# q and k of the first two units: vector-engine transposes replaced by tensor-engine transposes in a chunk attention + gated MLP kernel

## The chip, the cores and the metric

The kernel runs on one core of one Trainium2 chip. The metric is the device time of one execution in microseconds (us). The engines are TensorE (PE; PEld is its weight load), VectorE (DVE), ScalarE (ACT), GpSimd (POOL) and SyncE (SP). SP and POOL issue the DMAs here: SP on queue q1, POOL on queue q0.

## The reference

Chunk attention without a causal mask over chunks of 64 positions, then a two-layer MLP with a swish that has its own beta for each hidden unit. Batch 8, 8 heads, 576 positions, head size 64; 4608 tokens, model width 512, hidden width 2048, all float32.

```python
scores = scale * np.matmul(q_c, k_c.transpose(0, 1, 2, 4, 3))   # (B, H, 9, 64, 64)
scores = scores - np.max(scores, axis=-1, keepdims=True)
attn = np.exp(scores)
attn = attn / (np.sum(attn, axis=-1, keepdims=True) + 1e-09)
out = np.matmul(attn, v_c)
...
x = np.ascontiguousarray(attn_out.transpose(0, 2, 1, 3)).reshape(B * S, H * D)
h = x @ w_in
g = h * (1.0 / (1.0 + np.exp(-beta * h)))
return (g @ w_out).astype(np.float32)
```

## The kernel before

**Units and blocks.** The 4608 tokens are cut into 18 units of 256, and two units make a block of 512 for the MLP. A unit goes through these steps: load q, k and v (all converted to float16); transpose q and k, so that the head dimension lies in the partitions; scores in PSUM (a tile `sc`); exponential on ScalarE (`et`, L208 for units 0 and 1); product with v, which carries a column of ones so that the row sum comes with it (`emit_pv`, L266); reciprocal and multiplication on VectorE (`emit_norm`, L285 and L287); TensorE transposes of the normalized output into `xp` (L303), and a copy to `xt` (L304). `emit_m` (L329, L339, L343) then makes one of 16 hidden pieces of 128: four matmuls into `hps`, a tanh on ScalarE into `sg`, and one VectorE instruction that makes `gt` from both (a swish written with a tanh). `emit_t` (L361, L371) multiplies `gt` with w_out, and the result goes out.

**Order.** The order of each engine's instructions is the order of the calls in the text, written out by hand; each engine runs its own in order, and waits are set by the framework from the tiles that are read and written. PSUM tiles come from three pools: `ps_p`, four banks in turn (tag "p"), and `ps_s` and `ps_x`, two banks each, one tile at a time (tags "s" and "x").

**Units 0 and 1** are treated apart, since nothing else can run until they are done. Their q and k are loaded together, 512 tokens, four tokens to a partition, and by halves of the heads (a = 0 and 1, four heads each). Half 0 comes on SP's queue as float32 (`raw0`) and is cast on ScalarE (L178); half 1 comes on POOL's queue, which converts it to float16 (`qk0[1]`, named h in the profile). `emit_T_half` (L174) transposes with VectorE, which works on 32x32 blocks; taken on pairs of float16, this leaves 32 partitions with two interleaved elements, so `emit_sc_half` (L186) needs two accumulating matmuls over 32 rows for each score tile of 64x64: 32 matmuls for a unit and a half. `emit_ex_half` (L206) takes the exponential. After half 0 of unit 0, the scores of both units' other halves follow, then `emit_pv(0)` and `emit_pv(1)`, and the first pieces of `emit_m` on columns 0 to 256 (the tokens of unit 0), four of them, with the transposes of unit 1's output in between. Then the same four pieces on columns 256 to 512 (unit 1), and from there pieces of 512 columns. `gt` of these first pieces is made where the calls `vec()` stand.

**Fillers.** `emit_tiny` and `emit_idle` are matmuls on zeros that only keep TensorE busy. One matmul reads `late`, which POOL sets after two loads of v, so that the fillers behind it don't start before that.

**POOL's queue** is issued in this order: q and k of half 1 (L401), v in pieces of 128 tokens (L113; pieces 0 and 1 belong to unit 0, 2 and 3 to unit 1), the identity for the TensorE transposes (two POOL instructions in masks.py), eight pieces of w_in (L131), w_out (L137) and then unit after unit. An issue waits until the one eight before it has landed. **SP's queue**: q and k of half 0 (L401), beta in four pieces (L407), and later the outputs.

**Unit 2** is placed in the second layer of block 0, which runs as 16 chunks (i) of four matmuls each: its scores ahead of chunk 8, its product ahead of chunk 10, the transposes of its output ahead of chunk 13.

Of the kernel before, what the change touches and what calls it, by code (L numbers as in the profile page):

```python
# [8 lines left out]
FP32 = mybir.dt.float32  # L9
# [6 lines left out]
def kernel(  # L16
# [45 lines left out]
    qkT0 = [[const.tile([128, HH, 128, 2], FP16, name=f"t0{i}{a}") for i in range(2)] for a in range(2)]  # L62
# [111 lines left out]
    def emit_T_half(a):  # L174
        for i, h0, h1 in ((0, 0, HH), (1, 0, HH // 2), (1, HH // 2, HH)) if a == 0 else ((0, 0, HH), (1, 0, HH)):
            src = qk0[a][i][:, h0:h1]
            if a == 0:
                nc.scalar.copy(out=src, in_=raw0[i][:, h0:h1])  # L178
            nc.vector.transpose(
                out=qkT0[a][i][:, h0:h1].rearrange("p h s e -> p (h s e)").bitcast(FP32).rearrange(  # L180
                    "p (h i r) -> p h r i", h=h1 - h0, r=4),
                in_=src.rearrange("p h r d -> p (h r d)").bitcast(FP32).rearrange(
                    "p (h r i) -> p h r i", h=h1 - h0, r=4),
            )

    def emit_sc_half(u, a):  # L186
# [5 lines left out]
        qt, kt = qkT0[a]  # L192
        for h in range(HH):
            for e in range(2):
                for s in range(2):
                    p0 = 64 * u + 32 * s
                    for c in range(2):
                        nc.tensor.matmul(  # L198
                            out=sc[64 * c:64 * c + 64, s, HH * a + h, :],
                            lhsT=kt[p0:p0 + 32, h, 64 * c:64 * c + 64, e],  # L200
                            rhs=qt[p0:p0 + 32, h, 64 * c:64 * c + 64, e],
                            start=(e == 0),
                            stop=(e == 1),
                        )

    def emit_ex_half(u, a, n=1):  # L206
        hs = slice(HH * a, HH * (a + n))
        nc.scalar.activation(  # L208
            out=et_t[u][:, :, hs], in_=x_t["sc", u][:, :, hs], func=ACTF.Exp, scale=scale)
# [44 lines left out]
    def emit_pv(u, where=("x", "s")):  # L254
        et = et_t.pop(u)
        for s in (1, 0) if u >= MU else (0, 1):
# [137 lines left out]
    with tc.manual_schedule():  # L394
# [13 lines left out]
        for i in range(4):  # L408
            load_v(i)
            if i == 1:  # L410
                nc.gpsimd.memset(late, 0.0)
        nxt[0] = 2
        make_identity(nc, ident)
        for g in range(8):
            load_w_in(g)
# [230 lines left out]
```

The softmax here doesn't subtract the row's maximum and nothing guards it: scores larger than these inputs give would overflow.

## Time and profile before

| | us |
|---|---|
| median of 12 runs | 288.13 |
| lowest, highest | 287.24, 289.14 |
| profiled execution, its own time | 287.64 |
| its span in the profile | 285.9 |

The span runs from the first instruction of the program to the last that the profiler recorded, and is 1.74 us shorter than the execution's own time. Times inside the profile are us from the start of the span. A line of the timeline has start, length, engine, line of the kernel, operation, the tile written and the tiles read, the shape, the number of instructions that were merged, and in brackets how long the engine stood idle before it and what ended that. The chain of waits is the work that ended last, followed back from the end; its lines have start, length, engine, tile and line. In the DMA view a line for a queue has packets, megabytes, and the time of its packets as a share of the 16 DMA engines' time in the window.

### The profile page before, as it was taken

The numbers are of one execution on the slowest core, as the hardware profiler recorded it, in microseconds if no ns is written. First come the engines' busy times: TensorE is split into PE (matmuls) and PEld (weight loads), VectorE is DVE, ScalarE is ACT, GpSimd is POOL, SyncE is SP. The second block draws the span as 40 slices with busy tenths as digits, with TensorE's granted clock in tenths as the row PEclk, the third lists the DMA queues.
The fourth block names the chain that finished last, engine by engine and source line by source line (L and its number), as shares of the span: only waits on it lengthen the run. The fifth ranks groups of instructions, "written<-read, shape, count | busy, mean of one in ns | idle before, by whom it ended". The sixth has DMA issues, their size and how long they took to land.

```text
span 285.9 us, 6671 instructions
## 1 busy us (share of the span) xinstructions
PE 279.0 (98%) x2779; PEld 136.1 (48%) x2779; DVE 143.9 (50%) x268; ACT 146.3 (51%) x223; POOL 95.7 (33%) x125
## 2 busy tenths in 40 slices
PE   6989999999999999999999999999999999999995
PEld 3564456544544444444444444444444444444444
DVE  2778444776558553535454536363635463333301
ACT  4478228773557545455554555554645444444411
POOL 8853678488073991258627000000000000000000
PEclk9999999999999999999999999999999999999999
DMA  8999999999999999999999993425311221010012
GB/s 194 176 197 206 181 180 213 209 166 149 205 96 185 177 176 175 159 145 175 197 161 177 156 169 78 100 57 119 86 48 39 73 57 55 37 39 37 37 73 76
DMA packets 141085, 37.40 MB, mean 131 GB/s; under 512 B 128000, under 2 KB 136576, under 8 KB 141056
## 3 DMA queue, kind: packets, MB, share of 16 engines
q0 software_dynamic: 99136, 17.83, 79.0%
q1 hardware_dynamic: 41776, 19.09, 33.2%
q8 instruction: 22, 0.36, 0.5%
q10 hardware_dynamic: 144, 0.07, 0.1%
q14 instruction: 7, 0.06, 0.1%
HBM read 36.71 MB, written 9.44 MB: 161 GB/s over the span
## 4 chain that ended last, share of the span: by engine, by line
PE 94%; DMA 3%; ACT 1%; issue 1%; DVE 0%; POOL 0%; DVEq 0%; POOLq 0%
PE hps L329 44%; PE ops L361 43%; DMA h<-in_k_dram 3%; PE x L266 2%; PE sc L238 1%; PE ops L602 1%; PE sc L225 1%; PE y L266 1%; ACT xt L304 1%; PE xp L303 0%; PE sc L198 0%; ACT et L208 0%; POOL h L401 0%; PE warm L381 0%; PE xp L311 0%
## 5 line engine op out<-in xcount | busy, mean ns | idle before, releaser
L343 DVE SCALAR_TENSOR_TENSOR gt<-sg,hps 128x512 f16<-128x512 f32 (+1 forms) x153 | 99.2, 655 | 102.0 <-ACT sg L339 101.2
L329 PE MATMUL hps<-xt,win 128*128 128x512 f16 (+1 forms) x612 | 136.2, 367 | 0.8 <-ACT xt L304 0.7
L339 ACT ACTIVATE sg<-hps,beta 128x512 f32<-128x512 f32 (+1 forms) x153 | 100.4, 663 | 71.2 <-PE hps L329 69.5
L361 PE MATMUL ops<-wout,gt 128*128 128x512 f16 x560 | 131.1, 379 | 0.0
L329 PEld LDWEIGHTS <-win 128*128 128x128 f16 x612 | 58.1, 98 | 62.7 <-issue 1.4
L361 PEld LDWEIGHTS <-gt 128*128 128x128 f16 x560 | 54.1, 98 | 64.1
L371 ACT ACTIVATE osb<-ops 128x512 f32<-128x512 f32 x35 | 20.9, 598 | 42.7 <-PE ops L361 42.7
L113 POOL DMA_DIRECT2D vbig<-in_v_dram x40 | 34.1, 868 | 12.0 <-DMA qu<-in_q_dram 4.7
L99 POOL DMA_DIRECT2D qu<-in_q_dram x22 | 18.7, 859 | 25.9 <-DMA qT<-qu 23.6
L287 DVE TENSOR_TENSOR x<-x,rd 128x512 f16<-128x512 f32 x27 | 18.7, 691 | 1.0
L99 POOL DMA_DIRECT2D ku<-in_k_dram x22 | 18.7, 871 | 1.0 <-DMA ku<-in_k_dram 0.9
L285 DVE RECIPROCAL rd<-x 128x8 f32<-128x8 f32 x27 | 5.4, 199 | 12.6 <-PE x L266 12.6
L247 ACT ACTIVATE et<-sc 128x1024 f16<-128x1024 f32 (+1 forms) x8 | 6.4, 811 | 8.8 <-PE sc L238 8.7
L231 ACT ACTIVATE et<-sc 128x1024 f16<-128x1024 f32 x10 | 10.2, 1022 | 0.8 <-PE sc L225 0.2
L266 PEld LDWEIGHTS <-et 64*64 64x64 f16 x576 | 6.0, 107 | 7.4 <-issue 4.7
L287 DVE TENSOR_TENSOR x<-y,rd 128x256 f16<-128x256 f32 x18 | 7.6, 424 | 0.6
L381 PE MATMUL warm<-idle 128*128 128x512 f16 (+1 forms) x32 | 7.8, 396 | 0.0
L105 POOL DMA_DIRECT2D qu<-in_q_dram x9 | 6.8, 769 | 2.3 <-DMA vbig<-in_v_dram 0.8
L105 POOL DMA_DIRECT2D ku<-in_k_dram x9 | 6.8, 762 | 1.8 <-DMA win<-in_moe_w_in_dram 1.3
L266 PE MATMUL x<-vbig,et 64*64 64x65 f16 x432 | 6.7, 194 | 0.2 <-ACT et L208 0.2
L614 DVE TENSOR_SCALAR osb<-ops 128x256 f32<-128x256 f32 (+1 forms) x2 | 0.7, 358 | 12.1 <-PE ops L602 12.1
L131 POOL DMA_DIRECT2D win<-in_moe_w_in_dram x8 | 6.0, 758 | 1.2 <-DMA vbig<-in_v_dram 0.9
(46 smaller groups left out, 75.1 us busy)
## 6 DMA issues: line engine op xcount, KB each, us to landing
out_dram<-osb SPq DMA_DIRECT2D x35, 256.0 KB, 2.9
vbig<-in_v_dram POOLq DMA_DIRECT2D x32, 128.0 KB, 8.1
qu<-in_q_dram POOLq DMA_DIRECT2D x20, 128.0 KB, 6.2
ku<-in_k_dram POOLq DMA_DIRECT2D x20, 128.0 KB, 7.7
win<-in_moe_w_in_dram POOLq DMA_DIRECT2D x8, 256.0 KB, 8.8
wout<-in_moe_w_out_dram POOLq DMA_DIRECT2D x4, 512.0 KB, 12.5
qu<-in_q_dram POOLq DMA_DIRECT2D x3, 256.0 KB, 7.2
ku<-in_k_dram POOLq DMA_DIRECT2D x3, 256.0 KB, 7.8
```

Source lines behind the costliest of these rows:

```text
L99: nc.gpsimd.dma_start(out=tv[off:off + n, sp], in_=src[b, :, s:s + n, :].rearrange("h p d -> p h d"),)
L105: nc.gpsimd.dma_start(out=t[off // 2:(off + n) // 2], in_=src[b, :, s:s + n, :].rearrange("h (p r) d -> p h r d", r=2),)
L113: nc.gpsimd.dma_start(out=vbig[off:off + n, i, :, 0:D], in_=v[b, :, s:s + n, :].rearrange("h p d -> p h d"),)
L231: nc.scalar.activation(out=et, in_=sc, func=ACTF.Exp, scale=scale)
L266: nc.tensor.matmul(out=(x[0][64 * c:64 * c + 64, r, g, 0:D + 1] if len(x) == 1 else x[r][64 * c:64 * c + 64, g, 0:D + 1]), lhsT=(et[64 * r ...
L287: nc.vector.tensor_tensor(out=o, in0=z[..., 0:D], in1=rd[:, r].to_broadcast(list(o.shape)), op=ALU.mult)
L329: nc.tensor.matmul(out=hps[:, 0:n], lhsT=w_in16[m // 2][:, kk, (m % 2) * 128:(m % 2) * 128 + 128], rhs=xr[:, c0 // CH:(c0 + n) // CH, 2 * ...
L339: nc.scalar.activation(out=sg[:, 0:n], in_=hps[:, 0:n], func=ACTF.Tanh, scale=beta2[:, m:m + 1])
L343: nc.vector.scalar_tensor_tensor(out=gt_t[j][:, m, c0:c0 + n], in0=sg[:, 0:n], scalar=1.0, in1=hps[:, 0:n], op0=ALU.add, op1=ALU.mult,)
L361: nc.tensor.matmul(out=ops, lhsT=gt_t[j][:, kk, t * 128:(t + 1) * 128], rhs=w_out16[kk // 4][:, kk % 4, :], start=(kk == 0), stop=(kk == K ...
L371: nc.scalar.activation(out=osb, in_=ops, func=ACTF.Copy, scale=0.5)
L381: nc.tensor.matmul(out=d[:, 0:w], lhsT=idle[:, 0:128], rhs=idle[:, 0:w])
```

## The change

q and k of units 0 and 1 are transposed on TensorE, against the identity, one head and one of the four token positions at a time: 16 transposes of 128 x 64 for each of q and k and each half of the heads, 64 in all, into a PSUM tile `tq` that fills one bank. Even heads go to partitions 0 to 63, odd ones to 64 to 127. Two copies bring a tile to SBUF and put the tokens in order on the way: ScalarE takes heads 0 and 1 of the half (f = 0), VectorE heads 2 and 3 (f = 1). The casts of half 0 are shared in the same way. The scores need one matmul over 64 rows for each tile, 16 for a unit and a half instead of 32. `et` of units 0 and 1 is then ordered as it already is in units 8 and up, which `emit_pv` is told.

The identity is made first on POOL, `late` is set after one load of v instead of two, and piece 0 of w_in is issued ahead of v of unit 1. The fillers are placed anew. The product of unit 1 is split: its first part (s = 0) ahead of the first hidden pieces, its second part behind two of them; all four `vec()` of the first pieces now stand behind the transposes of unit 1's output. Unit 2's scores and product stand one chunk later (9 and 11).

```diff
--- before.py
+++ after.py
@@ -59,7 +59,7 @@
     HH = H // 2
     raw0 = [const.tile([128, HH, 4, D], FP32, name=f"raw{i}") for i in range(2)]
     qk0 = [[const.tile([128, HH, 4, D], FP16, name=f"h0{i}{a}") for i in range(2)] for a in range(2)]
-    qkT0 = [[const.tile([128, HH, 128, 2], FP16, name=f"t0{i}{a}") for i in range(2)] for a in range(2)]
+    qkT0 = [[const.tile([128, 2, 128, 4], FP16, name=f"t0{i}{a}") for i in range(2)] for a in range(2)]
     braw = const.tile([128, 32], FP32)
     gate = const.tile([128, 1], FP16)
     bt = const.tile([128, 32], FP32)
@@ -171,17 +171,25 @@
     x16_t = {}
     xt_t = {}
 
-    def emit_T_half(a):
-        for i, h0, h1 in ((0, 0, HH), (1, 0, HH // 2), (1, HH // 2, HH)) if a == 0 else ((0, 0, HH), (1, 0, HH)):
-            src = qk0[a][i][:, h0:h1]
-            if a == 0:
-                nc.scalar.copy(out=src, in_=raw0[i][:, h0:h1])
-            nc.vector.transpose(
-                out=qkT0[a][i][:, h0:h1].rearrange("p h s e -> p (h s e)").bitcast(FP32).rearrange(
-                    "p (h i r) -> p h r i", h=h1 - h0, r=4),
-                in_=src.rearrange("p h r d -> p (h r d)").bitcast(FP32).rearrange(
-                    "p (h r i) -> p h r i", h=h1 - h0, r=4),
-            )
+    tq_t = {}
+
+    def emit_cast_half(i, f, cast):
+        hs = slice(2 * f, 2 * f + 2)
+        cast(out=qk0[0][i][:, hs], in_=raw0[i][:, hs])
+
+    def emit_T_half(a, i):
+        z = tq_t[a, i] = ps_p.tile([128, 2, 4, 128], FP16, tag="p", name="tq")
+        for h in range(HH):
+            p0 = 64 * (h % 2)
+            for r in range(4):
+                nc.tensor.transpose(
+                    out=z[p0:p0 + 64, h // 2, r, :], in_=qk0[a][i][:, h, r, :], identity=ident)
+
+    def emit_cp_half(a, i, f, copy):
+        copy(
+            out=qkT0[a][i][:, f],
+            in_=tq_t[a, i][:, f].rearrange("p r t -> p t r"),
+        )
 
     def emit_sc_half(u, a):
         if a == 0:
@@ -189,24 +197,22 @@
             pool, tag = ((ps_s, "s"), (ps_x, "x"))[u]
             x_t["sc", u] = pool.tile([128, 2, H, CH], FP32, tag=tag, name="sc")
         sc = x_t["sc", u]
-        qt, kt = qkT0[a]
-        for h in range(HH):
-            for e in range(2):
-                for s in range(2):
-                    p0 = 64 * u + 32 * s
+        qt, kt = (z.rearrange("p g t r -> p g (t r)") for z in qkT0[a])
+        for s in range(2):
+            for g in range(2):
+                for par in range(2):
                     for c in range(2):
+                        t0 = UNIT * u + 128 * s + 64 * c
                         nc.tensor.matmul(
-                            out=sc[64 * c:64 * c + 64, s, HH * a + h, :],
-                            lhsT=kt[p0:p0 + 32, h, 64 * c:64 * c + 64, e],
-                            rhs=qt[p0:p0 + 32, h, 64 * c:64 * c + 64, e],
-                            start=(e == 0),
-                            stop=(e == 1),
+                            out=sc[64 * c:64 * c + 64, par, 4 * s + 2 * a + g, :],
+                            lhsT=kt[64 * par:64 * par + 64, g, t0:t0 + 64],
+                            rhs=qt[64 * par:64 * par + 64, g, t0:t0 + 64],
                         )
 
     def emit_ex_half(u, a, n=1):
-        hs = slice(HH * a, HH * (a + n))
-        nc.scalar.activation(
-            out=et_t[u][:, :, hs], in_=x_t["sc", u][:, :, hs], func=ACTF.Exp, scale=scale)
+        o, i = ((z.rearrange("p e (s g) q -> p (e s) g q", s=2)[:, :, 2 * a:2 * a + 2] if n == 1 else z)
+                for z in (et_t[u], x_t["sc", u]))
+        nc.scalar.activation(out=o, in_=i, func=ACTF.Exp, scale=scale)
 
     ex_t = {}
 
@@ -251,9 +257,9 @@
         while ex_t[u] and not later:
             emit_ex(u)
 
-    def emit_pv(u, where=("x", "s")):
-        et = et_t.pop(u)
-        for s in (1, 0) if u >= MU else (0, 1):
+    def emit_pv(u, where=("x", "s"), which=None):
+        et = et_t[u]
+        for s in which or ((1, 0) if u >= MU else (0, 1)):
             i = 2 * u + s
             if where[s] == "p":
                 x = [ps_p.tile([128, 4, 128], FP32, tag="p", name=f"y{r}") for r in range(2)]
@@ -266,7 +272,7 @@
                         nc.tensor.matmul(
                             out=(x[0][64 * c:64 * c + 64, r, g, 0:D + 1] if len(x) == 1 else
                                  x[r][64 * c:64 * c + 64, g, 0:D + 1]),
-                            lhsT=(et[64 * r:64 * r + 64, s, 4 * c + g, :] if u < XU else
+                            lhsT=(et[64 * r:64 * r + 64, s, 4 * c + g, :] if 2 <= u < XU else
                                   et[64 * r:64 * r + 64, g % 2, 4 * s + 2 * c + g // 2, :]),
                             rhs=vbig[64 * r:64 * r + 64, i, 4 * c + g, 0:D + 1],
                         )
@@ -297,7 +303,7 @@
 
     def emit_xt_pe(u, s, copy=nc.scalar.copy):
         xf = x16_t.pop((u, s)).rearrange("p r h d -> p (r h d)")
-        tag = "s" if u < 2 and (u, s) != (1, 0) else "xp"[s]
+        tag = ("ss", "sx")[u][s] if u < 2 else "xp"[s]
         xp = {"x": ps_x, "s": ps_s, "p": ps_p}[tag].tile([128, 4, 128], FP16, tag=tag, name="xp")
         for g in range(4):
             nc.tensor.transpose(out=xp[:, g, :], in_=xf[:, g * 128:(g + 1) * 128], identity=ident)
@@ -396,6 +402,7 @@
         nc.vector.memset(idle, 0.0)
         nc.vector.memset(braw, 0.0)
         nc.vector.memset(vbig[:, :, :, D:D + 1], 1.0)
+        make_identity(nc, ident)
         for a, eng, dst in ((0, nc.sync, raw0), (1, nc.gpsimd, qk0[1])):
             for i, src in enumerate((q, k)):
                 eng.dma_start(
@@ -405,13 +412,14 @@
         bv = moe_beta.rearrange("(m w f) -> w m f", w=4, f=32)
         for w in range(4):
             nc.sync.dma_start(out=braw[32 * w:32 * w + KFF, :], in_=bv[w])
-        for i in range(4):
-            load_v(i)
-            if i == 1:
-                nc.gpsimd.memset(late, 0.0)
+        load_v(0)
+        nc.gpsimd.memset(late, 0.0)
+        load_v(1)
+        load_w_in(0)
+        load_v(2)
+        load_v(3)
         nxt[0] = 2
-        make_identity(nc, ident)
-        for g in range(8):
+        for g in range(1, 8):
             load_w_in(g)
         for g in range(3):
             load_w_out(g)
@@ -419,47 +427,62 @@
         load_w_out(3)
         loads_to(3)
 
-        emit_tiny(78)
+        emit_tiny(75)
+        act_cp, vec_cp = nc.scalar.copy, nc.vector.tensor_copy
+        warm = idle_bank()
+        emit_idle(6, 512, warm)
+        nc.tensor.matmul(out=warm[:, 0:16], lhsT=idle[:, 0:128], rhs=late)
+        emit_idle(1, 512, warm)
+        for i in range(2):
+            emit_cast_half(i, 0, act_cp)
+            emit_cast_half(i, 1, vec_cp)
+        for i in range(2):
+            emit_T_half(0, i)
+            emit_cp_half(0, i, 0, act_cp)
+            emit_cp_half(0, i, 1, vec_cp)
+            if i == 0:
+                emit_idle(2, 512, warm)
+        emit_T_half(1, 0)
+        emit_cp_half(1, 0, 0, act_cp)
+        emit_cp_half(1, 0, 1, vec_cp)
+        emit_idle(1, 512, warm)
+        emit_sc_half(0, 0)
+        emit_ex_half(0, 0)
+        emit_sc_half(1, 0)
+        emit_T_half(1, 1)
+        emit_cp_half(1, 1, 0, act_cp)
+        emit_cp_half(1, 1, 1, vec_cp)
         warm = idle_bank()
         emit_idle(3, 512, warm)
-        nc.tensor.matmul(out=warm[:, 0:16], lhsT=idle[:, 0:128], rhs=late)
-        emit_idle(8, 512, warm)
-        emit_T_half(0)
-        emit_sc_half(0, 0)
-        emit_ex_half(0, 0)
-        warm = idle_bank()
-        emit_idle(6, 512, warm)
-        emit_T_half(1)
         nc.vector.transpose(out=bt, in_=braw)
         emit_sc_half(0, 1)
         emit_ex_half(0, 1)
-        emit_sc_half(1, 0)
+        emit_sc_half(1, 1)
+        emit_ex_half(1, 0, 2)
+        nc.scalar.activation(out=beta2, in_=bt[:, 0:KFF], func=ACTF.Copy, scale=0.5)
         emit_idle(2, 512, warm)
+        emit_idle(10, 64, warm)
         loads_to(5)
         emit_pv(0, ("s", "p"))
-        emit_sc_half(1, 1)
-        emit_ex_half(1, 0, 2)
         emit_norm(0, 0)
         emit_norm(0, 1)
-        emit_idle(1, 512, warm)
-        emit_idle(12, 64, warm)
+        emit_idle(4, 512, warm)
         emit_xt_pe(0, 0)
-        emit_pv(1, ("x", "p"))
-        emit_norm(1, 1)
+        emit_idle(4, 512, warm)
+        emit_xt_pe(0, 1)
+        emit_pv(1, ("p", "x"), (0,))
         emit_norm(1, 0)
-        nc.scalar.activation(out=beta2, in_=bt[:, 0:KFF], func=ACTF.Copy, scale=0.5)
-        emit_xt_pe(0, 1)
         d = [emit_m(0, m, 0, 256, True) for m in (0, 1)]
         d[0][0]()
-        emit_xt_pe(1, 1)
+        emit_pv(1, ("p", "x"), (1,))
+        emit_norm(1, 1)
         d[1][0]()
-        d.append(emit_m(0, 2, 0, 256, True))
-        d[0][1]()
-        emit_xt_pe(1, 0, nc.vector.tensor_copy)
-        d.append(emit_m(0, 3, 0, 256, True))
+        emit_xt_pe(1, 0)
+        d += [emit_m(0, m, 0, 256, True) for m in (2, 3)]
+        emit_xt_pe(1, 1, vec_cp)
         for act, _ in d[2:]:
             act()
-        for _, vec in d[1:]:
+        for _, vec in d:
             vec()
         for m in range(4):
             emit_m(0, m, 256, 256)
@@ -467,9 +490,9 @@
             emit_m(0, m)
         emit_T(2)
         for i in range(16):
-            if i == 8:
+            if i == 9:
                 emit_sc(2)
-            if i == 10:
+            if i == 11:
                 emit_pv(2)
                 emit_norm(2, 0)
                 emit_norm(2, 1)
```

## The prediction

> **What bounds the kernel now.** I read the page's head first, then the chain of waits over the first 30 us, then the timeline of the same stretch, then the DMA view by windows.
>
> From the page:
>
> ```profile
> span 285.9 us, 6671 instructions
> PE 279.0 (98%) x2779; PEld 136.1 (48%) x2779; DVE 143.9 (50%) x268; ACT 146.3 (51%) x223; POOL 95.7 (33%) x125
> ```
>
> TensorE is the bound, and its few idle times lie at the start: after its first instruction at 0.96 us it stands still for 2.6 us in all, 0.1 us of it after 17.6. So what counts is when TensorE begins to stream without a break. The chain of waits (start, length, what) shows that:
>
> ```profile
> 2.13 7.17 DMA h<-in_k_dram
> ...
> 10.46 0.71 PE sc L198 x62
> ...
> 15.14 1.03 PE hps L329 x8
> ...
> 17.57 12.28 PE hps L329 x64
> ```
>
> The last load of the first heads, h of k, lands at 9.30; scores start at 10.46, the first hidden layer (hps, L329) at 15.14, and from 17.57, the first of the 256:512 pieces (call it the stream), nothing stops TensorE. The work behind that point is the same in both kernels, so the change moves the end by what it moves 17.57. The prices come from the timeline (start, length, engine, line):
>
> ```profile
> 4.85 3.58 PE L381 MATMUL warm<-idle 128*128 128x512 f16 x8
> 6.11 1.14 ACT L178 CAST h<-raw 128x512 f16<-128x512 f32 x2 [0.44 <-DMA raw<-in_k_dram]
> 8.73 1.47 PE L381 MATMUL warm<-idle 128*128 128x512 f16 x6
> 9.32 1.09 DVE L179 STREAM_TRANSPOSE t<-h 128x512 f32<-128x512 f32 x1 [0.24 <-DMA h<-in_k_dram]
> 10.97 0.60 ACT L208 ACTIVATE et<-sc 128x512 f16<-128x512 f32 x1 [1.51 <-PE sc L198]
> 11.64 0.32 PE L266 MATMUL x<-vbig,et 64*64 64x65 f16 x16
> 13.01 0.40 PE L303 MATMUL xp<-ident,x 128*128 128x128 f16 x4
> 13.45 0.58 ACT L304 COPY xt<-xp 128x512 f16<-128x512 f16 x1
> 15.43 0.69 DVE L287 TENSOR_TENSOR x<-x,rd 128x512 f16<-128x512 f32 x1
> 16.67 0.39 PE L303 MATMUL xp<-ident,x 128*128 128x128 f16 x4
> 17.09 0.42 DVE L304 COPY xt<-xp 128x512 f16<-128x512 f16 x1 [0.33 <-PE xp L303]
> 17.43 3.03 DVE L343 SCALAR_TENSOR_TENSOR gt<-sg,hps 128x256 f16<-128x256 f32 x7
> ```
>
> **The loads.** Between 1.5 and 4.9 us the DMA view knows one queue only, that of the raw loads:
>
> ```profile
> q1 hardware_dynamic: 941, 0.95, 84.6%
> ```
>
> The h loads were issued at 1.24 and 2.13, yet not one of their packets ran by then. The change puts the identity ahead of them on POOL; its two instructions took 6.38 to 6.97, 0.59 us, so the h issues come at most 0.59 later. At 119.88, a later q load issued after its queue had run empty had its first packet by 122.41: 2.54 us. Then 1.83 + 2.54 = 4.37 is still inside the time of the raw loads, so I take 0, hidden by those; if the 3.69 us from issue to first packet were all the queue's own, it is +0.59. w_in piece 0 moves past the two v loads of unit 1: those land later (12.79 was the last; the 256 KB ahead of it cost 1.3, as between the landings at 14.09 and 15.42), 14.1 at worst, but are first used near 15.6. Piece 0 landed before its use already: 0 gained, and without that cover a late v would hold unit 1's products by its lateness. SP's queue is as before.
>
> **Up to the exponentials of unit 0's second half.** Before: landing 9.30, one DVE transpose 1.09, exp at 10.97, so 1.67 after the landing. The rest of the DVE transposes lay under the load. After: TensorE transposes, 16 of 64 columns a tile; four xp transposes took 0.40 and start 0.056 apart, so 16 take 15 x 0.056 + 0.22 = 1.06. Then two copies. The changed program's order has VectorE's copy wait for ScalarE's copy of the same tile, so they stand in line: 0.58 (the xt copy, same shape) plus, on VectorE, 0.42 (same shape, but contiguous) to 0.69 (512 results at L287's pace). The copy reads at a stride of 128 elements, so I take 0.69. Each hand-over costs about 0.03 to 0.05.
>
> TensorE is in order, and ahead of the last transposes stand both first-half scores, which need all of the raw k path: raw k lands 6.08, ScalarE's cast ends 6.72 (0.62 each; VectorE's half beside it), transposes 7.85, copies 8.45 and 9.2, 32 score tiles 0.3 (16 small matmuls of L266 take 0.32, starts over 0.15): 9.5. The transposes of k's last half run 9.5 to 10.56, copies to 11.2 and 11.9, its scores to 12.25, exp at 12.28. That is **+1.31**. On ScalarE the first exp (0.60) stands between these copies, from 9.65, behind the copy of h of q, to 10.3, so it is out of the way at 10.56; behind VectorE's waiting copy stand only the transpose of beta and the normalizing, not yet due. The bounds: with the two column groups overlapping (0.62 for 16) and 0.42 on VectorE, scores are out of the way at 8.8 and exp comes at 11.4, +0.4; with +0.59 on the load, 12.6, +1.7. Nothing waits for the transpose of beta until the first tanh.
>
> **From exp to the stream.** Exp 0.60, then pv of unit 0: before 10.97 to 11.64. In between the change has scores of unit 1 and fillers, 0.15 + 2 x 0.216 + 10 x 0.03 = 0.9 from 12.03: done at 12.9, just under 12.95. Then rec, multiply, xp, copy to xt, twice, to the first hps: 11.64 to 15.14, 3.50, which the change keeps (the eight fillers, 0.86 for each four, end about when VectorE does). First hps: 16.45. Behind that it is longer. Before, the products of unit 1 were done ahead of the first hps, and 17.57 came 2.43 later. After, two hidden pieces, 8 x 0.109 = 0.87, precede the second product; then 0.38 to its rec (11.64 to 12.02), 0.92 rec and multiply (15.20 to 16.12), 0.05 and 0.42 for xp (16.67 to 17.09), and copy plus the first gt, 0.76 (17.09 to 17.85), since all gt now stand behind that copy on VectorE and the stream's first bank is the first gt's: 3.4. **+1.0**, bounds +0.6 (no wait for gt) to +1.2.
>
> Sum: 1.31 + 1.0 = 2.3 on the profiled execution's own 287.64: 289.95. That execution was 0.49 under the median 288.13 of its runs. With the same distance 290.4; the new warm-up has no hole at 3.58, so a little of that distance may go: **290.3**. Pushing sc and pv of unit 2 one chunk back costs nothing: its kT and qT were ready at 35.7, 1.0 ahead, and a later stream adds to that; xp of unit 2 then follows pv by two chunks, 1.73 + 0.37 = 2.10, against 1.31 and 2.15 for the two multiplies (39.16 to 40.47 and 41.31), and the second is wanted 0.2 later. Without that cover, 0.3.
>
> **The clock.** Eight fillers from 4.85 took 3.58, six from 8.73 took 1.47: starts 0.43 and 0.216 apart, so the clock doubled near 8.3, after 3.5 us without a hole. After, the fillers run from 2.1 to 5.1 and then come transposes, so the sum above takes it as doubled by 7. Should it come only at 7.8, the raw k path is 0.5 later. If transposes did not bring it up at all, each 16 cost 1.8: 5.27, 7.05, fillers, 9.7, 11.5, 14.1, copies 15.5, exp 16.1, +5.1, and the halved pace of fillers and the first pieces another 1 to 2. No row of before shows a transpose on a slow clock.
>
> [...]
>
> **Rivals.** (1) The slow clock, 295: the transposes begin before the clock has risen, and nearly half of TensorE's time from 5.3 to 10 is theirs; against it, the fillers without a hole. (2) Cheap prices: column groups overlap, contiguous pace on VectorE, and v, issued later, leaves h of k its engines, so that it lands a microsecond sooner, 8.3. The first-half scores stand ahead until 8.8, so exp comes at 10.9 (8.8 and 2.1 of the low prices), -0.1, and the tail costs its low 0.6: +0.5, 288.6, no change. Speaking for it: 128-byte packets of v run beside the last of h. (3) The other side: the landing of h of k moves far more. With the low prices exp is 2.1 after the landing, so the shift is landing + 2.1 - 10.97 + 0.9 = landing - 7.97, and the kernel is faster by more than 0.2% when h of k lands before 7.4, with raw k a microsecond sooner too; at 7.3 it gives 287.4. Against it: the raw and h loads read 2 MB, which at the 331 to 369 GB/s of the DMA view from 3 to 5.2 us need about 6 us from 2.0 on, and the change takes no byte away.
>
> **Numbers.** Forecast 0.74 (own range 289.0 to 292.0), slow clock 0.12, no change 0.07, faster 0.07. About 0.2% (0.58 us) is what the runs can tell from no change. The range of 288.4 to 292.5 holds the forecast with its bounds and the case of cheap prices, and leaves out the slow clock above and the faster case below, 0.19. Slower 0.74 + 0.12 = 0.86, same 0.07, faster 0.07.
>
> **What would show it.** VectorE's tq copy starting when ScalarE's ends, 0.6 to 0.7 long; exp of unit 0's second half near 12.3; first hps near 16.4; the stream near 19.9, waiting for gt behind the xt copy; the granted clock up by 7. h of k landing away from 9.3, or transposes spaced by 0.11, would make it wrong.

## The result and the profile after

The changed kernel took 291.04 us (median of 11 runs, 290.13 to 293.30) against 287.90 us for the kernel before, measured beside it (47 runs, 287.15 to 290.51): a ratio of 1.0112, 95% interval 1.0093 to 1.0132. It is slower by 3.1 us; the forecast was 290.3, in a range of 288.4 to 292.5.

The execution that was profiled is the longest of the eleven, 293.30 us. So it shows the change together with something that most of the other runs don't have, and the two must be taken apart. First the head of its page (engine, busy us, share, instructions):

```profile
span 291.5 us, 6669 instructions
PE 283.4 (97%) x2777; PEld 139.0 (48%) x2777; DVE 143.4 (49%) x269; ACT 147.7 (51%) x226; POOL 95.8 (33%) x125
```

The span grew by 5.6 us, TensorE's busy time by 4.4: TensorE did not only wait more, it was also busy longer, with almost the same number of instructions. Next the chain of waits of the changed kernel over the first 24 us (start, length, what):

```profile
1.44 8.28 DMA h<-in_q_dram
9.72 0.04 issue
9.77 1.08 PE tq L185 x16
...
14.35 0.62 PE sc L206 x21
...
19.75 1.03 PE hps L335 x8
...
22.51 0.42 DVE xt L310
22.93 0.34 DVE gt L349
23.27 0.05 issue
23.32 0.72 PE hps L335 x5
```

Three things are to be seen. h of q now stands in the chain and lands at 9.72 (before: 7.96); h of k lands at 11.06 (before: 9.30). The first hidden layer comes at 19.75 instead of 15.14. The stream, which began at 17.57, begins at 23.32, and what holds it back at the last is VectorE's copy of xt and behind it the first gt. From there TensorE needs 264.9 us to its last matmul, before 265.0: all of the loss lies ahead of the stream.

The windows view of the same kernel, cut where the granted clock changes (stretch, length, busy us with the number of instructions, the clock as PEclk):

```profile
core 0: us, PE busy (x) PEld busy (x) DVE busy (x) ACT busy (x) POOL busy (x), PEclk, DMA share, GB/s
5.70:9.12 3.42, 1.64 (x32) 0.89 (x26) 2.07 (x3) 1.69 (x3) 2.46 (x3) 1.00 1.37 150
9.12:15.95 6.83, 6.18 (x106) 3.62 (x107) 1.50 (x3) 2.91 (x5) 4.46 (x6) 0.50 1.89 177
```

The clock rose at 5.71, as forecast: there the trace's record of the clock begins, and the fillers, 0.43 us apart from 2.07 on, are 0.22 apart from 6.07 on (the first two lines of the next view). Then TensorE stood still from 7.43 to 9.77, waiting for h of q, the clock was halved at 9.12 and came back only at 15.95, just before the products of unit 0. All that TensorE did between the landing of h and those products ran at half pace. Of the eleven runs, the three with a mean clock of 0.993 or less took 292.2 to 293.3; the eight others took 290.1 to 291.4, with a median of 290.8. That is the change without this accident: 2.9 us above the kernel before. Of the three only this one has a profile, so what went with the lower clock is seen for it alone.

The timeline shows the price of the new work at both clocks, and how the copies stand (start, length, engine, line; in brackets the idle time before and what ended it):

```profile
2.07 2.74 PE L387 MATMUL warm<-idle 128*128 128x512 f16 x6
...
6.07 0.61 PE L387 MATMUL warm<-idle 128*128 128x512 f16 x2
...
6.77 0.66 PE L185 MATMUL tq<-ident,h 128*64 128x128 f16 x16
...
11.88 1.07 PE L185 MATMUL tq<-ident,h 128*64 128x128 f16 x16
...
13.01 0.59 ACT L189 COPY t<-tq 128x512 f16<-128x512 f16 x1 [0.62 <-PE tq L185]
13.63 0.69 DVE L189 COPY t<-tq 128x512 f16<-128x512 f16 x1 [1.42 <-ACT t L189]
```

Sixteen transposes take 0.66 us, or 1.07 on the halved clock. VectorE's copy starts at 13.63, when ScalarE's has ended (13.60), and is released by it: the two stand in line, 0.59 and 0.69 us.

### The profile page after: what moved, and what is told of

It reads as the page before. It is cut to its first block, busy times and chain, and to the rows that moved or that the text cites. A ratio compares the mean times of both kernels' runs of the same rounds, so it can differ in the third digit from the quotient of the medians.

```text
span 291.5 us, 6669 instructions
## 1 busy us (share of the span) xinstructions
PE 283.4 (97%) x2777; PEld 139.0 (48%) x2777; DVE 143.4 (49%) x269; ACT 147.7 (51%) x226; POOL 95.8 (33%) x125
## 4 chain that ended last, share of the span: by engine, by line
PE 94%; DMA 3%; ACT 1%; issue 0%; DVE 0%; POOL 0%; POOLq 0%; DVEq 0%
PE hps L335 43%; PE ops L367 42%; DMA h<-in_q_dram 3%; PE warm L387 2%; PE x L272 2%; PE sc L244 1%; PE ops L625 1%; PE sc L231 1%; PE tq L185 1%; PE y L272 1%; ACT xt L310 1%; PE xp L309 1%; PE sc L206 0%; PE xp L317 0%; DVE xt L310 0%
## 5 line engine op out<-in xcount | busy, mean ns | idle before, releaser
L387 PE MATMUL warm<-idle 128*128 128x512 f16 (+1 forms) x33 | 9.3, 425 | 0.0
```

The source lines that it names most:

```text
L387: nc.tensor.matmul(out=d[:, 0:w], lhsT=idle[:, 0:128], rhs=idle[:, 0:w])
```

## The experiments

The theory going in: about 1 us is lost in the tail between the first hidden layer and the stream, an estimated 0.8 us because two copies of one PSUM tile stand in line, the rest on the way over TensorE. Its rivals: the dropped clock is most of it, or the load order on POOL is. Each kernel was measured beside the kernel before; the ratios are to that, and a difference of two ratios is turned into us by taking it times 288. Where a run's mean clock is 0.994 or less, as in the three above, it is counted among those with a dropped clock; the others are called undisturbed.

**Fillers over the hole.** The changed kernel, with something for TensorE to do while h of q is late:

```
+        emit_idle(8, 512, warm)
         emit_T_half(1, 0)
```

> The changed kernel with eight more filler matmuls (512 columns) ahead of the transposes of q's second half, where its profile shows TensorE idle from 7.43 to 9.77 and the granted clock halved from 9.12 to 15.95. Theory (the chain of transposes and copies, +1.3, and the longer tail, +1.0, make most of the loss; the dropped clock makes the rest, about 0.9 of the 3.1 us): the clock stays up once it has risen, and the time falls by 0.5 to 1.2 us against the changed kernel, to about 290. Rival (the dropped clock is most of the loss): it falls by 2 us or more, to 289 or less. Rival (late loads of q and k alone): no change, 291.

Measured: 291.69 us (4 runs), ratio 1.0132 [1.0117, 1.0147]. In its profile the clock rises at 5.31 and never drops. But nothing was gained, and the chain of waits says why:

```profile
6.76 0.66 PE tq L185 x16
7.42 1.83 PE warm L387 x8
9.26 0.59 PE tq L185 x16
```

In this execution h of q had landed at 8.19; the fillers held TensorE until 9.25, and the transposes queued behind them. Fillers long enough for a late landing cost a microsecond at an early one. So neither the time of the theory (290) nor that of its first rival (289) came. That the drop is not most of the 3.1 us is what the eight undisturbed runs of the changed kernel say; this cure is no better than the drop, with intervals that overlap.

**The tail in the old order.** From the first output transposes to the stream, the order of before: products and normalizing of unit 1 ahead of the first hidden layer, gt between the copies of xt:

```
-        emit_idle(4, 512, warm)
+        emit_pv(1, ("x", "p"))
+        emit_norm(1, 1)
+        emit_norm(1, 0)
+        emit_idle(2, 512, warm)
         emit_xt_pe(0, 1)
-        emit_pv(1, ("p", "x"), (0,))
-        emit_norm(1, 0)
...
+        emit_xt_pe(1, 1)
...
-        emit_xt_pe(1, 0)
-        d += [emit_m(0, m, 0, 256, True) for m in (2, 3)]
-        emit_xt_pe(1, 1, vec_cp)
+        d.append(emit_m(0, 2, 0, 256, True))
+        d[0][1]()
+        emit_xt_pe(1, 0, vec_cp)
+        d.append(emit_m(0, 3, 0, 256, True))
...
```

> The changed kernel with the order of the kernel before from the first output transposes to the stream: both products of unit 1 ahead of the first hidden pieces, and gt of piece 0 ahead of the last copy to xt on VectorE. Theory: the stretch from the first hidden piece to the stream goes back from 3.57 to about 2.4, the gap before the stream that waits for gt (0.85) is gone, and the time falls by about 1.0 us, to about 290. Rival (the tail is covered by something else, for instance the first hidden piece then comes later by as much because the second product now stands in VectorE's way): 0 to 0.3.

Measured: 290.31 us (6 runs), ratio 1.0091 [1.0071, 1.0111]. The chain of waits of this kernel:

```profile
17.23 1.03 PE hps L335 x8
...
19.19 0.43 DVE xt L310
19.62 0.05 issue
19.67 1.38 PE hps L335 x11
```

From the first hidden layer to the stream it is 2.44 us instead of 3.57, and no gt stands between the copy and the stream. 1.13 us are saved here by the profiles. A little of it is given back, as the rival had it: from the exponential of unit 0's second half to the first hidden layer it is 4.49 us here (12.74 to 17.23), against 4.35 and 4.36 in three profiles with the new tail. The ratios show 0.6, and their intervals overlap.

**Two PSUM tiles for a transposed half.** So that the copies need not wait for one another:

```
-        z = tq_t[a, i] = ps_p.tile([128, 2, 4, 128], FP16, tag="p", name="tq")
+        z = tq_t[a, i] = [ps_p.tile([128, 4, 128], FP16, tag="p", name=f"tq{f}") for f in range(2)]
...
-                emit_idle(2, 512, warm)
+                emit_idle(2, 512)
...
-        emit_idle(1, 512, warm)
+        emit_idle(1, 512)
...
```

Three of the fillers get PSUM tiles of their own with it.

> The changed kernel with each transposed tile split over two PSUM tiles, one for each copy, so that VectorE's copy no longer waits for ScalarE's. Theory: the two copies run side by side, 0.69 instead of 1.3 from the transposes to the scores; the time falls by 0.5 to 0.9 us. Rival (the copies lie beside a load or a filler that ends later): no change within 0.3.

Measured: 290.30 us (6 runs), ratio 1.0090 [1.0069, 1.0111]. The timeline of this kernel:

```profile
10.18 0.58 ACT L189 COPY t<-tq 128x512 f16<-128x512 f16 x1
10.40 0.69 DVE L189 COPY t<-tq 128x512 f16<-128x512 f16 x1 [0.68 <-PE tq L185]
```

Both copies are released by TensorE and run beside one another, at the same lengths as before. From the landing of h of k to the exponential of unit 0's second half it is 1.84 us here, against 2.57 in the kernel with the old tail, whose copies stand in line (10.17 to 12.74). The ratio is 0.6 us under that of the changed kernel, and again the intervals overlap.

**The POOL order alone, in the kernel before.** Identity first, late after the first v, first w_in piece after the second:

```
+        make_identity(nc, ident)
         for a, eng, dst in ((0, nc.sync, raw0), (1, nc.gpsimd, qk0[1])):
...
-        for i in range(4):
-            load_v(i)
-            if i == 1:
-                nc.gpsimd.memset(late, 0.0)
+        load_v(0)
+        nc.gpsimd.memset(late, 0.0)
+        load_v(1)
+        load_w_in(0)
+        load_v(2)
+        load_v(3)
...
-        make_identity(nc, ident)
-        for g in range(8):
+        for g in range(1, 8):
```

> The kernel before with nothing but the changed order on POOL's queue: identity first, late behind one load of v, piece 0 of w_in ahead of v of unit 1. Theory: the h loads land where they did (9.3 for k, within 0.3), and the time is that of before within 0.4 us. Rival (the order on POOL made the loads late: the changed kernel's profile has q of the second half landing at 9.72 and k at 11.06, against 7.96 and 9.30): both land 1.5 us later here too, and the time is 1.0 to 1.8 us above before.

Measured: 289.12 us (12 runs), ratio 1.0057 [1.0033, 1.0081], 1.6 us by the ratio. This was the surprise: an order of issue that the prediction had at nothing. But half of the 1.6 us is the clock: four of the twelve runs have a mean clock of 0.986 to 0.994 and took 290.5 to 291.7, the eight others 288.2 to 289.2, with a median 0.8 us above the kernel before. In the profile, an undisturbed run, h of k lands at 9.69, and yet the chain of waits goes through v of unit 1, which lands at 14.41, to the stream at 18.21 (before: 17.57):

```profile
6.47 7.95 DMA vbig<-in_v_dram
...
14.46 0.32 PE y L266 x16
...
18.21 3.86 PE hps L329 x25
```

The order was split in two.

**The identity alone ahead of the h loads, in the kernel before.**

```
+        make_identity(nc, ident)
         for a, eng, dst in ((0, nc.sync, raw0), (1, nc.gpsimd, qk0[1])):
...
         nxt[0] = 2
-        make_identity(nc, ident)
```

> The kernel before with the identity ahead of the h issues on POOL and nothing else changed (late and w_in as before). The kernel before with the whole new POOL order had a ratio of 1.0057. Theory (the identity puts off the h issues by some 0.2 us and all landings behind them): ratio 1.001 to 1.003, h of k landing 9.5. Rival (the identity is the whole of it): 1.005. Rival (it is the 256 KB of w_in that shares the DMA engines): 1.000.

Measured: 288.65 us (10 runs), ratio 1.0027 [1.0014, 1.0040], 0.8 us, and no run with a dropped clock; h of k lands at 9.72, and the stream begins at 18.18. That the landing alone makes the 0.8 us is not shown. `late` is set 0.2 us later here too, and in this profile the clock rises at 9.81 (before: 8.34), so that the fillers end at 10.91, beside VectorE's last transpose (10.87), and either of them would hold the scores:

```profile
9.13 1.78 PE L381 MATMUL warm<-idle 128*128 128x512 f16 x6
...
10.69 0.18 DVE L433 STREAM_TRANSPOSE bt<-braw 128x32 f32<-128x32 f32 x1
...
10.90 0.71 PE L198 MATMUL sc<-t,t 32*64 32x64 f16 x64
```

**The w_in piece alone, in the kernel before.**

```
             if i == 1:
                 nc.gpsimd.memset(late, 0.0)
+                load_w_in(0)
...
-        for g in range(8):
+        for g in range(1, 8):
             load_w_in(g)
```

> The kernel before with the first w_in piece ahead of the v loads of unit 1 on POOL and nothing else changed. Theory (v of unit 1 lands up to 1.3 us later and is wanted near 12.4, when the products of unit 1 are due in this kernel): ratio 1.002 to 1.004, a wait of TensorE for v ahead of the products of unit 1. Rival (it is hidden): 1.000. Rival (h of k lands later beside it): h of k after 9.6 and a ratio of 1.005.

Measured: 288.38 us (11 runs), ratio 1.0026 [1.0013, 1.0039]; h of k lands at 8.72. Its timeline shows the wait for v that the first theory asked for:

```profile
14.38 0.32 PE L266 MATMUL y<-vbig,et 64*64 64x65 f16 x16 [0.21 <-DMA vbig<-in_v_dram]
```

Here the stream begins at 18.14. By the ratios the two halves add to 1.5 us, and the whole was 1.6; but that they add is not shown. The whole has the four runs with a dropped clock (the identity alone has none, the w_in piece alone two of eleven), and in the profiles the stream comes 0.61 and 0.57 us later by the halves and 0.64 by both: the wait for v covers what h is late. In the profile of the changed kernel the v of unit 1 is wanted only at 19.0, so the second half has no such wait there.

**The old POOL order in the changed kernel.** The h loads first, then the identity, the four v loads, all of w_in:

```
-        make_identity(nc, ident)
         for a, eng, dst in ((0, nc.sync, raw0), (1, nc.gpsimd, qk0[1])):
...
-        load_v(0)
+        make_identity(nc, ident)
         nc.gpsimd.memset(late, 0.0)
-        load_v(1)
-        load_w_in(0)
-        load_v(2)
-        load_v(3)
+        for i in range(4):
+            load_v(i)
...
```

> The changed kernel with the load order of before: h of q and h of k issued first on POOL, then the identity, then the four v loads, then all of w_in. Theory (the new order on POOL costs about a microsecond in either kernel, by landing h later): 289.8 to 290.2, ratio about 1.007, h of k landing near 9.3 and first hps about a microsecond before that of the changed kernel. Rival (in the changed kernel the transposes and copies of the raw k path end last, so that the landing of h is covered): no change from 291.0, ratio 1.011.

Measured: 290.24 us (6 runs), ratio 1.0088 [1.0072, 1.0104]; h of k lands at 9.24. This is the kernel that the prediction's sum described, with the loads where it put them, and its chain of waits goes through that sum's steps one by one:

```profile
1.27 5.44 DMA raw<-in_k_dram
...
6.73 0.63 ACT h L178
...
7.40 0.68 PE tq L185 x16
...
8.10 0.59 ACT t L189
...
8.72 0.70 DVE t L189
...
9.47 0.41 PE sc L206 x28
9.88 0.61 PE tq L185 x16
...
10.52 0.59 ACT t L189
...
11.13 0.70 DVE t L189
...
11.88 0.41 PE sc L206 x28
12.29 0.83 PE warm L387 x12
...
16.58 1.03 PE hps L335 x8
...
20.15 3.86 PE hps L335 x25
```

The chain starts at raw k, not at h of k: cast, transposes, two copies in line, first-half scores, and only then the transposes of h of k, though that had landed 0.6 us earlier. In the profiles with the new order and no long fillers the chain starts at h of q instead, which lands at 8.28 to 9.72, against 7.82 here. The run undoes the identity, `late` and the w_in piece together; which of them counts in the changed kernel was not tested.

**All three undone.** Two tiles, the old tail and the old POOL order (the diffs above together); what is left of the change is TensorE's transposes with 64x64 score tiles.

> The changed kernel with three parts undone at once: the two copies of a tile from two PSUM tiles so that they run side by side, the tail from the first output transposes to the stream in the order of before, and the load order of before on POOL. What is left of the change is the TensorE transposes with the 64x64 score tiles. Theory (the three parts add up: 0.7, 0.7 and about 1): 288.4 to 288.9, ratio 1.002 to 1.004, stream near 18. Rival (they hide one another, the last of them setting the end): 289.6 to 290.0, ratio about 1.007.

Measured: 289.20 us (5 runs), ratio 1.0046 [1.0033, 1.0058]. Undone singly, the three gave 0.60, 0.63 and 0.69 us by the ratios, and together 1.90. A part of each is the clock, since three of the changed kernel's eleven runs have it dropped, one of six with the old tail, and none of the other three kernels. By medians of the undisturbed runs, each against the kernel before beside it, the three give 0.49, 0.42 and 0.34 us, and together 1.38. Either way they add, as far as the noise allows: each single interval still overlaps that of the changed kernel, and the joint one is clear of it. Some 1.3 us stay (1.5 by medians), more than the theory had left. h of k landed at 8.64 here, and yet the products of unit 0 start at 12.39, because of a pause that no wait explains, in the chain of waits of this kernel:

```profile
10.77 0.65 PE warm L387 x6
11.42 0.70 issue
12.12 0.33 PE warm L387 x6
```

TensorE stops in the middle of ten like fillers. The next kernels went after that pause.

**One long filler instead of ten short ones** (in the kernel with all three undone):

```
-        emit_idle(10, 64, warm)
+        emit_idle(1, 512, warm)
```

> The kernel with the three parts undone, and its ten 64-column fillers ahead of the products of unit 0 replaced by one of 512 columns: the same TensorE time (0.22 against 0.28 us), 18 instructions fewer. In the profile of the kernel with the ten, TensorE stood still for 0.70 us in the middle of them, waiting for nothing that is shown. Theory (the pause comes with the many short instructions): the pause goes and the products of unit 0 start 0.7 to 0.9 us sooner: 288.3 to 288.6, ratio 1.002. Rival (an accident of that one profile): no change, 289.2, ratio 1.0046, and no pause in this profile either. Rival (what is left is the path over transposes and copies itself): 289.0 to 289.2 with the pause still there.

Measured: 288.88 us (8 runs), ratio 1.0040 [1.0024, 1.0056]. The interval overlaps that of the kernel with the ten, so a gain is not shown. The pause has not gone but moved into the products of unit 0, and is shorter, in a profile that is the fastest of the eight executions (288.20):

```profile
11.47 0.15 PE x L272 x3
11.62 0.22 issue
11.84 0.29 PE x L272 x13
```

**Fewer instructions at the start** (in the kernel with all three undone):

```
-        emit_tiny(75)
+        emit_tiny(43)
...
-        emit_idle(6, 512, warm)
+        emit_idle(7, 512, warm)
```

> The kernel with the three parts undone, and at its very start 43 tiny matmuls instead of 75 and seven 512-column fillers instead of six: about the same TensorE time, some 60 instructions fewer ahead of everything. Theory (the 0.70 us pause stands at a fixed number of instructions, where the supply of instructions is late): it moves some 60 instructions further on, into a time where TensorE waits anyway or out of the short instructions: 288.4 to 288.8. Rival (no supply of instructions is involved): no change from 289.2, ratio 1.0046.

Measured: 291.13 us (6 runs), ratio 1.0105 [1.0071, 1.0139]. The time went the other way, in part by the clock: three of the six runs have a mean clock of 0.988 to 0.994 and took 291.8 to 292.2, the others 289.2 to 290.5, the profiled one 289.71. But the place is the one that the theory named: the pause moved on by some 60 instructions, into the second half of the first products.

```profile
11.81 0.08 PE y L272 x9
11.89 2.00 issue
13.89 0.25 PE y L272 x7
```

Counting TensorE's records in the three traces (weight loads, matmuls and the few others that it has), the pause stands between the 449th and the 450th in every one, whatever the instructions there are. Each of the three is one execution; how long the pause is in the others is not known. And it ends 2.2 to 2.5 us after a 16 KB packet of the queue that the DMA view calls "instruction" began to move: 9.95 and 12.12, 9.32 and 11.84, 11.51 and 13.89.

**More instructions at the start** (from the kernel with the one long filler):

```
-        emit_tiny(75)
+        emit_tiny(107)
...
-        emit_idle(6, 512, warm)
+        emit_idle(5, 512, warm)
```

> The kernel with the three parts undone and the one 512-column filler, and at its very start 107 tiny matmuls instead of 75 and five 512-column fillers instead of six: about the same TensorE time, some 60 instructions more. In the three profiles of this family the pause stood at the same place of TensorE's record count, between the 449th and the 450th record, 0.22 to 2.00 us long, and ended 2.2 to 2.5 us after a 16 KB packet of the instruction queue had begun to move (9.95, 9.32, 11.51); that packet began 3.7 to 4.1 us after the 193rd record, 256 records earlier. Theory (the packet is asked for near the 193rd record and then stands behind the loads of h): with 64 records more at the start the 193rd falls near 2.3 us instead of 5.7, the packet moves before 6, no pause is seen at the 450th record, and the time is 288.2 to 288.5, ratio 1.0015 to 1.002. Rival (the packet is tied to the end of the h loads whenever it is asked for): it begins near 9.5 again, and the time stays at 288.9 or rises, since the 450th record comes sooner.

Measured: 289.68 us (6 runs), ratio 1.0070 [1.0054, 1.0086]. Two halves of the theory part here. The packet moves at 5.28, and the 449th and 450th record follow one another without a pause, as it said. This is the DMA view of the stretch from 5 to 6 us (queue, packets, MB, share):

```profile
q8 instruction: 1, 0.02, 6.2%
```

But the time rose. With that packet among the h loads, h of q lands at 8.34 and h of k at 9.45, against 7.25 and 8.76 in the profile of the kernel it was made from, and the chain of waits now starts at h of q. The pause is given back as a later landing, by these two profiles; that the packet is what makes the loads late is not shown by them.

**The identity between the h loads and the v loads, in the kernel before** (late after the first v):

```
+        make_identity(nc, ident)
         for i in range(4):
             load_v(i)
-            if i == 1:
+            if i == 0:
                 nc.gpsimd.memset(late, 0.0)
         nxt[0] = 2
-        make_identity(nc, ident)
```

> The kernel before with the identity between the h issues and the v loads on POOL, and late after the first v load, so that late lands when it did. In the two runs with this order h of k landed at 8.64 and 9.24 and v of unit 0 no later than 10.91. Theory (v issued 0.6 us later leaves h of k the engines): h of k lands near 8.9 and the time is 287.3 to 287.6, ratio 0.998 to 0.999. Rival (the landing of h is bound by its own bytes, and differs from run to run by as much): ratio 1.000 within 0.0015.

Measured: 287.69 us (12 runs), ratio 0.9998 [0.9987, 1.0008]; h of k lands at 9.15. No gain. In this profile the theory could not show itself: the clock rises at 10.54, and the scores wait for fillers until 10.94, though VectorE had done h of k at 10.29. No version measured here beats the kernel before.

## The prediction, step by step

The direction was right, and so was the reason: TensorE's path from the load to the stream got longer in two places, and nothing behind the stream changed (264.9 us to the last matmul, before 265.0). The median is 0.7 us above the forecast, the undisturbed runs 0.5; as a rise over the kernel before, 2.2 us were forecast (290.3 against 288.13) and 3.1 measured. Of its own signs of being wrong one came: h of k landed at 11.06, away from 9.3. The times that it named for the first hidden layer and the stream (16.4, 19.9) were 19.75 and 23.32 in the profile of the changed kernel, and 16.58 and 20.15 with the old load order.

**The loads.** This step failed. The prediction took 0 for the identity ahead of the h loads, hidden by the raw loads, with +0.59 as its bound; even that bound is under what the landings show. The h issue comes 0.20 us later (1.44 instead of 1.24) and the first packet of that queue hardly later (4.94 to 5.20 us in six profiles with the identity first, 4.91 to 5.16 in eight with the h issues first). So at the first packet the cover seems to hold. But the queue's 300th packet comes at 6.35 to 6.52 against 6.03 to 6.13, and h of k lands at 9.58, 9.65, 9.69, 9.72, 10.17, 11.06 against 8.64, 8.72, 8.75, 8.76, 9.15, 9.24, 9.30, 9.45: the two sets don't overlap, and their medians are 0.75 us apart. Undoing the order in the changed kernel gave 0.69 us by the ratios, 0.34 by undisturbed medians, and there it is h of q that the chain starts from. Why 0.2 us of issue become 0.75 us of landing is open. The v loads behind w_in did land late, at 15.77 where the prediction had 14.1 at worst, and cost nothing in the changed kernel, as it said.

**The prices.** VectorE's copy at 0.69 us and ScalarE's at 0.58 to 0.59, in line, are as forecast. The transposes were mis-sized: 0.66 us for sixteen, not 1.06; the bound with overlapping column groups (0.62) was the nearer one. In the profile of the changed kernel the sixteen from 6.77 on start in eight pairs, 0.01 to 0.03 us apart in a pair and 0.06 to 0.08 from pair to pair; that the two of a pair are of different column groups no view names. That it changed little is luck: raw k landed at 6.71 in the profile with the old load order, the latest of all fourteen (the prediction had 6.08), and two transposes, each 0.4 cheaper, and a load 0.63 later nearly cancel.

**Up to the exponential, +1.31.** With the loads where the prediction had them, the first-half scores began at 9.47 and were done near 9.9, and the exponential of unit 0's second half came at 12.22; the prediction had those scores done at 9.5 and the exponential at 12.28. So the time fits, by the path that was named, with the two errors above in it.

**To the first hidden layer.** The scores of unit 1 and the fillers were to end just under the exponential; they end after it, and the products come 0.83 us after its start (12.22 and 13.05 with the old load order) instead of 0.67. From the products to the first hidden layer it was 3.50, to be kept: the changed kernel has 3.52, with the clock up again since 15.95.

**The tail, +1.0.** It took 3.57 us, 1.14 more than before, nearly the upper bound of 1.2, in this and three other profiles (3.57 to 3.58), and by the wait that was named: the gt behind the copy of xt.

**The clock.** "Doubled by 7" held, at 5.71 (in the profile with the old tail, with the same start, it was 7.37). What the prediction had not seen is a second drop, at 9.12, while TensorE stood still for h of q (7.43 to 9.77). Its slow-clock rival put 295 on a halved clock, and the profiled run, with its clock halved for a while (0.50 from 9.12 to 15.95), took 293.3; but the cause it named is another: transposes that keep the clock from rising. In that profile the clock rose at 5.71 while the first sixteen transposes ran (5.29 to 6.13). Whether transposes alone would bring it up no run shows, since fillers run ahead of them (from 2.07). What dropped it is not shown either: in the 3.41 us before the drop TensorE was busy 1.64 us with transposes and fillers together, and stood still for 1.69. In the run with the fillers over the hole the same transposes ran and the clock stayed up, in all four executions (mean clock 0.999 to 1.000).

**PSUM.** The forecast had the two copies of a tile in line, and from one tile they were (ScalarE's to 13.60, VectorE's from 13.63). From two tiles they ran together (10.18 and 10.40), and 0.6 us was measured for that by the ratios, 0.4 by undisturbed medians. Both engines reading one tile at once was not tried.

**The other rivals.** Of the cheap prices one came true, the transposes; VectorE's contiguous pace did not (0.69 us, not 0.42), and h of k came later, not sooner (11.06, before 9.30). The case of a faster kernel asked for h of k before 7.4; the earliest landing in any profile was 8.64.

The sum: the run with the old load order stands at 290.24 us where the forecast for just that case was 290.3, and its stream at 20.15 where the forecast had 19.88; that it is so near is owed in part to the two errors that cancel. The undisturbed runs of the changed kernel have 290.8, which leaves 0.3 to 0.5 us for the load order, and the dropped clock lifts the median to 291.04.

## What to carry to other kernels

Don't take an instruction ahead of a load on the critical path for free because the queue seems covered: in this kernel two short ones moved the issue by 0.20 us and came with a landing 0.75 us later, and the first packet did not show it. A copy split over two engines gained here when each half had a tile of its own (1.84 against 2.57 us from landing to exponential). A filler against a late load is a bet on the landing: without one the clock dropped in three of eleven runs (mean clock 0.993 or less), and with eight the work waited a microsecond behind them (h of q landed at 8.19, and in the chain its transposes follow at 9.26). And before costs are added up, look at each run's clock: four runs with a dropped clock doubled what one order of loads seemed to cost (1.6 us instead of 0.8).

## What the hardware did that was not expected

TensorE stood still where the profile shows no wait, at one place of its record count. In all fourteen profiles a 16 KB packet of the instruction queue (on the page of the changed kernel 22 packets, 0.36 MB) moves 3.2 to 4.9 us after TensorE's 169th record. (That record was found afterwards, as about the one with the least spread; after the 193rd, which the last expectation took, it is 0.3 to 4.6 us.) And in the three where TensorE wanted its 450th record sooner than 2.2 to 2.5 us after that packet began, it stood still until then, for 0.70, 0.22 and 2.00 us, with no wait in the profile but "issue". In the kernel before and in the changed one the 450th record comes late enough (11.87 and 15.95, packets at 8.83 and 9.82), so this is no part of the 3.1 us; it is part of what stays when the rest is undone. That TensorE had run out of instructions there is the author's reading; it is not shown, since the view does not name the engine that a packet is for. An estimate from the three profiles: the stream begins at 18.48, 17.91 and 19.58, and if nothing else then held it, without the pause it would begin at 17.78, 17.69 and 17.58, against 17.57 before. So in them the pause is most of what stays, and the two extra hand-overs of the way over TensorE and PSUM the smaller part. By a run it is not settled: the one kernel of this family without a pause had its h loads later, with the stream at 18.31.
